# Regrouping the last stages of a fused attention and expert kernel: tiles 6, 7, 8 together, then 7, 8

## The chip, the cores and the metric

The kernel runs on 1 core of one Trainium2 chip. The metric is the device time of one execution in microseconds (us); lower is better. The engines are PE (matrix multiply, with its weight loads shown apart as PEld), DVE (vector), ACT (scalar), POOL (GpSimd) and SP, whose queue here only issues DMAs.

## What is computed

Three layers in float32, one after the other, on 1152 tokens (2 batches of 576) with 512 features:

```python
scores = scale * np.matmul(q, k.transpose(0, 1, 3, 2))          # 8 heads of 64
kth = np.partition(scores, -32, axis=-1)[..., -32:-31]           # the 32 largest of a row stay
attn = softmax(np.where(scores >= kth, scores, -1e9))
x = attn @ v
...
for e in range(4):                                               # all four experts, gated
    out += p[:, e:e + 1] * (np.maximum(x @ w1[e], 0.0) @ w2[e])
...
h = np.maximum(np.maximum(x @ w1, x @ w2), x @ w3)               # second network
return h @ w_out
```

The weights of the last network (m1, m2, m3, mo) arrive as float64 and are turned into float32 on the chip.

## The kernel before

The 1152 tokens are nine tiles of 128. Attention goes over 36 pairs (a tile and two heads), and a table of slots (`options`, constants FIRST, TIGHT and LOOSE at L35 to L37) says at which slot each step of a pair is issued: scores on PE, four rounds of MAX8 and MATCH_REPLACE8 on DVE, exp on ACT, masking on DVE or (pairs in ON_POOL) on POOL, transposes and the product with v on PE. Tiles 0 and 1 take whole float32 operands (`kfull`, `qfull`, and `first_alone` for the experts of tile 0); the later ones are split into a high and a low float32r part, and each product is three matmuls (`product`, L616 to L618).

Between these slots the generator `products` issues expert work. How much is issued after a slot is set by two counted clocks: the goal grows with the DVE time counted, times SHARE, and products are issued until PE's counted time has reached it. All engines take their instructions in the order in which they are written; nothing is reordered later.

Expert work goes by stages (`STAGES`). Stage c covers a short list of tiles and only half of the weights (`HALVES`: weight halves 0 to 3 in even stages, 4 to 7 in odd ones), so every tile stands in one even and one odd stage: stage 0 is tile 0 alone, stages 1 to 8 are [0, 1], [1, 2] to [7, 8], and stage 9 is tile 8 alone. One weight half of a stage is layer 1 (`half1`: 16 products, 48 matmuls, with as many columns as the stage has tokens), and one item later layer 2 (`half2`: 4 products, 12 matmuls of 512 columns for each tile). A stage thus needs 16 weight tiles of 512 KB. Each comes by a DMA on SP's queue into `raw` (3 buffers, L186), is rounded to `whi` by ACT (L235), and `wlo` is the difference, two POOL instructions, or from stage LATE = 8 on for every second tile one DVE instruction (L241). A stage can start when its newest tile has left attention.

From slot W_FROM = 306 on, when attention ends, the 48 pieces of the second network's weights are converted (`to_float32`: two ACT, three DVE and one POOL instruction, L206 to L218, then a DMA to DRAM, L223), one piece every two slots. The second network (`largest`) then takes three groups of three tiles; its weight tiles come from that DRAM copy (`raw<-narrow`), nine for its first layer (ps) and three for its second (pso).

The queue of SP also carries attention's loads: `qraw` (one buffer) and `kraw` (one buffer), each twice, L283.

The lines that set the stages:

```python
STAGES = [[0]] + [[t - 1, t] if t % RING else [t, t - 1] for t in range(1, NTILE)] + [[NTILE - 1]]
HALVES = [range(E) if not n % 2 else range(E, 2 * E) for n in range(len(STAGES))]
```

Of the kernel before, what the change touches and what calls it, by code (L numbers as in the profile page):

```python
# [22 lines left out]
RING = 4  # L23
# [7 lines left out]
ON_POOL = ((0, 1, 2, 3, 4, 5, 6, 7), (0, 1, 2, 3, 4, 5, 6))  # L31
W_FIRST, W_AHEAD = 60, 4
# [20 lines left out]
def kernel(  # L53
# [72 lines left out]
    def load_gates():  # L126
        nc.scalar.dma_start(out=gate, in_=gates)
# [178 lines left out]
    def load_q(c, hp):  # L306
        t = qraw[c, hp] = qp.tile([P, 2, WIDTH], F32, tag="qraw", bufs=1, name="qraw")
# [40 lines left out]
    class Pair:  # L348
# [136 lines left out]
        def split_x(self):  # L485
# [8 lines left out]
            at_ = self.t % RING * P  # L494
# [4 lines left out]
    def attention():  # L499
# [5 lines left out]
        def options(n):  # L505
            return FIRST if n < EARLY else TIGHT if n == EARLY else LOOSE
# [6 lines left out]
        for n, (c, hp, t) in enumerate(pairs):  # L513
# [8 lines left out]
            elif n:  # L522
                at_slot(8 * n + options(n)["scores"] - LOAD_FULL, load_full, n)
# [46 lines left out]
        for n in range(len(HALVES[0]) * 2 + 2):  # L570
# [114 lines left out]
    def first_alone():  # L685
# [3 lines left out]
        for e in range(len(HALVES[0]) // 2):  # L689
# [16 lines left out]
            load_alone(14 + 2 * e)  # L706
        flush()
        for e, h in hs.items():
            ps = po.tile([P, DM], F32, tag="o", name="ps2")
            for y in range(2):  # L710
                for u in range(2):
                    w = w_alone["b", 2 * e + y, u]
                    for f in range(2):
# [3 lines left out]
                        yield True  # L717
            later(gated(ps, 0, e, not e, False))
        flush()

    def experts():
# [29 lines left out]
        def half2(c, i, hs, ti):  # L751
            t = STAGES[c][ti]
            if not i % 2:
                outs[t] = po.tile([P, DM], F32, tag="o", name="ps2")
# [5 lines left out]
            new = c < NTILE and t == c  # L760
            if new and t not in accs:
                sums(t)
                first = True
            else:
                first = False
            later(*[lambda: None] * E_LAG, gated(ps, t, i // 2, first, not new and i == HALVES[c][-1]))

        before = None
        for c in range(1, len(STAGES)):
            phase[0] = c  # L770
            newest = min(c, NTILE - 1)
# [9 lines left out]
            for i in HALVES[c]:  # L781
# [6 lines left out]
                if i == HALVES[c][-1]:  # L788
                    x_free.update(t for t in STAGES[c] if t != c)
# [195 lines left out]
```

## Time and profile before

| what | us |
|---|---|
| median of 3 runs | 830.49 (830.01 to 836.0) |
| the profiled execution itself | 830.46 |
| its span, first to last instruction | 828.7 |
| PE busy | 766.3 (92%) |
| DVE busy | 664.5 (80%) |
| POOL busy | 580.5 (70%) |
| ACT busy | 492.8 (59%) |

The span is what the rows further down cut into stretches; the 1.8 us between it and the execution's time lie outside the instructions. Busy time of PE is that of overlapping matmuls, whose ends are modelled, so PE at 100% is not PE at its peak; for the pace of matmuls the starts are counted instead.

### The profile page before, as it was taken

To read this page: it belongs to the slowest core of one execution; us is meant where nothing else is said; L and a number is where in the kernel's file an instruction comes from. 1 tells how busy PE (TensorE), PEld (TensorE's weight loads), DVE (VectorE), ACT (ScalarE), POOL (GpSimd) and SP (SyncE) were. 2 spreads that over 40 slices of the span, in tenths; PEclk is the share of its full clock that TensorE was granted. 3 is DMA by queue.
4 is the path that set the end of the run, shared out by engine and by line. 5 is a ranking of instruction groups with operands and counts; after the bars stand their busy time and mean duration, and the time that the engine had idled before them with its cause. 6 is when DMAs were issued, how large, how long until landed. Compare 5 with 4: busy or idle time off the path is not lost. (4 is left out here: it accounts for less than half of the span.)

```text
span 828.7 us, 14306 instructions
## 1 busy us (share of the span) xinstructions
PE 766.3 (92%) x4950; PEld 675.6 (82%) x4950; DVE 664.5 (80%) x1226; ACT 492.8 (59%) x1046; POOL 580.5 (70%) x487
## 2 busy tenths in 40 slices
PE   5988899998999999999999999899999797899998
PEld 3667578887888999888998988688888696699996
DVE  6999698997789998988999987899986886144141
ACT  4566757784677676757777766556655643243341
POOL 2668858886898878869879868997876763163330
PEclk9889999999999999999999999999997899799999
DMA  7743525545546555445455436789878763452431
GB/s 212 217 135 124 151 75 160 170 131 163 151 129 185 151 156 163 118 128 163 141 161 149 147 120 203 230 255 286 279 242 277 249 212 105 165 193 87 153 114 39
DMA packets 58376, 138.58 MB, mean 167 GB/s; under 512 B 9984, under 2 KB 23296, under 8 KB 58304
## 3 DMA queue, kind: packets, MB, share of 16 engines
q1 hardware_dynamic: 49792, 128.93, 50.6%
q10 hardware_dynamic: 8512, 8.74, 3.0%
q8 instruction: 39, 0.64, 0.3%
q14 instruction: 33, 0.27, 0.1%
HBM read 128.99 MB, written 8.65 MB: 166 GB/s over the span
## 5 line engine op out<-in xcount | busy, mean ns | idle before, releaser
L241 POOL TENSOR_TENSOR wlo<-raw,whi 128x512 fp32r<-128x512 f32 x290 | 390.9, 1374 | 133.4 <-ACT whi L235 127.8
L235 ACT ACTIVATE whi<-raw 128x1024 fp32r<-128x1024 f32 x180 | 188.0, 1060 | 111.8 <-DMA raw<-in_w_dram 64.8
L616 PE MATMUL ps<-xl,whi 128*128 128x256 f32 (+2 forms) x648 | 190.5, 294 | 3.2 <-ACT r L461 3.2
L618 PE MATMUL ps<-xh,wlo 128*128 128x256 f32 (+2 forms) x648 | 188.1, 290 | 1.4 <-POOL wlo L241 1.4
L617 PE MATMUL ps<-xh,whi 128*128 128x256 f32 (+2 forms) x648 | 188.0, 290 | 0.0
L393 DVE MAX8 m<-work 128x8 f32<-128x576 f32 x216 | 154.7, 743 | 0.1
L616 PEld LDWEIGHTS ps<-xl,whi 128*128 128x128 f32 x648 | 123.7, 191 | 5.3 <-ACT r L461 3.9
L618 PEld LDWEIGHTS ps<-xh,wlo 128*128 128x128 f32 x648 | 124.1, 192 | 1.7 <-POOL wlo L241 1.7
L617 PEld LDWEIGHTS ps<-xh,whi 128*128 128x128 f32 x648 | 124.1, 191 | 1.0
L616 PE MATMUL ps<-wlo,h 128*128 128x512 f32 x272 | 111.9, 411 | 5.8 <-POOL wlo L241 4.0
L618 PE MATMUL ps<-whi,h 128*128 128x512 f32 x272 | 108.8, 400 | 2.8 <-POOL h L737 2.8
L241 DVE TENSOR_TENSOR wlo<-raw,whi 128x1024 fp32r<-128x1024 f32 x35 | 51.8, 1481 | 72.8 <-ACT whi L235 61.6
L617 PE MATMUL ps<-whi,h 128*128 128x512 f32 x272 | 108.1, 397 | 0.0
L395 DVE MATCH_REPLACE8 work<-m,work 128x576 f32<-128x576 f32 x144 | 106.5, 741 | 0.0
L616 PEld LDWEIGHTS ps<-wlo,h 128*128 128x128 f32 x272 | 52.4, 193 | 18.4 <-POOL wlo L241 6.4
L413 DVE SCALAR_TENSOR_TENSOR p<-s,m,p 128x576 f32<-128x576 f32 x57 | 66.9, 1174 | 0.0
L218 POOL TENSOR_TENSOR narrow<-narrow,raw 128x256 int32<-128x256 int32 x48 | 46.0, 961 | 29.2 <-issue 9.6
L618 PEld LDWEIGHTS ps<-whi,h 128*128 128x128 f32 x272 | 52.0, 191 | 16.3 <-POOL h L737 4.8
L380 ACT ACTIVATE s<-pss 128x288 f32<-128x288 f32 x144 | 51.6, 409 | 21.1 <-PE pss L373 11.1
L431 PE MATMUL psp<-ident,p 128*128 128x128 f32 x288 | 46.0, 284 | 15.4 <-DVE h L744 6.2
L617 PEld LDWEIGHTS ps<-whi,h 128*128 128x128 f32 x272 | 52.4, 192 | 8.8
L393 DVE MAX8 m<-s 128x8 f32<-128x576 f32 x72 | 54.1, 752 | 3.7 <-ACT rs L444 2.8
(97 smaller groups left out, 1515.8 us busy)
## 6 DMA issues: line engine op xcount, KB each, us to landing
raw<-in_w_dram SPq DMA_DIRECT2D x144, 512.0 KB, 4.0
raw<-narrow SPq DMA_DIRECT2D x36, 512.0 KB, 3.7
raw<-in_m_dram SPq DMA_DIRECT2D x36, 256.0 KB, 4.4
whole<-in_w_dram SPq DMA_DIRECT2D x16, 512.0 KB, 4.7
narrow<-narrow ACTq DMA_DIRECT2D x48, 128.0 KB, 3.7
kraw<-in_k_dram SPq DMA_DIRECT2D x16, 288.0 KB, 5.4
qraw<-in_q_dram SPq DMA_DIRECT2D x48, 64.0 KB, 2.5
raw<-in_mo_dram SPq DMA_DIRECT2D x12, 256.0 KB, 4.3
```

The source lines that it names most:

```text
L218: nc.gpsimd.tensor_tensor(out=out.bitcast(I32), in0=out.bitcast(I32), in1=last, op=ALU.add)
L235: nc.scalar.activation(out=hi, in_=raw, func=AF.Copy)
L241: on.tensor_tensor(out=lo[:, x], in0=raw[:, x], in1=hi[:, x].bitcast(F32), op=ALU.subtract)
L380: nc.scalar.activation(out=s[:, h, :], in_=halves[h][:, 0:SH], func=AF.Copy)
L393: nc.vector.max(m[:, 8 * r:8 * r + 8], src)
L395: nc.vector.match_replace(out=self.w[j], in_to_replace=m[:, 8 * r:8 * r + 8], in_values=src, imm_value=NEG)
L413: nc.vector.scalar_tensor_tensor(out=p, in0=s, scalar=kth, in1=p, op0=ALU.is_ge, op1=ALU.mult, accum_out=total)
L431: nc.tensor.transpose(ps[:, r * P:(r + 1) * P], self.p[:, part, part * TAIL + r * P:part * TAIL + (r + 1) * P], ident)
L616: nc.tensor.matmul(ps, lhsT=lh, rhs=rl, start=first, stop=False)
L617: nc.tensor.matmul(ps, lhsT=lh, rhs=rh, start=False, stop=False)
L618: nc.tensor.matmul(ps, lhsT=ll, rhs=rh, start=False, stop=last)
```

## The change

- Stages: 1 to 6 as before, then stage 7 is [6, 7, 8] and stage 8 is [7, 8]; stage 9 is gone. The slots of the ring that holds a tile's x move by one (`place`), so that the three tiles lie side by side. With three tiles a layer 1 pass is 384 columns wide and takes two PSUM banks, and the third output of layer 2 takes a bank of the same pool of six.
- The first stage's weights (`whole`): 13 instead of 10 are loaded ahead, three of them into the `raw` buffers; the rest, and the first loads and splits of stage 1, move from fixed slots into `first_alone`.
- `qraw` gets two buffers and shrinks from 384 to 256 columns a head.
- TIGHT is used for pairs 3 and 7 (before: 7 alone). The second head of pair 3 is masked on DVE, not POOL.
- SHARE is 1.0 throughout (before 1.03 from stage 2 on).
- Start: one DMA for q instead of two, the gates' DMA on SP, the ACT table load (`warm`) behind the first DMA issue.

```diff
-ON_POOL = ((0, 1, 2, 3, 4, 5, 6, 7), (0, 1, 2, 3, 4, 5, 6))
-W_FIRST, W_AHEAD = 60, 4
+ON_POOL = ((0, 1, 2, 3, 4, 5, 6, 7), (0, 1, 2, 4, 5, 6))
+W_AHEAD = 4
...
-SHARE, AHEAD = (1.0, 1.0, 1.03), 6
+SHARE, AHEAD = (1.0, 1.0, 1.0), 6
...
-PHASES = [(1, n) for n in range(10)] + [(2, 0), (2, 1), (2, 2)]
+PHASES = [(1, n) for n in range(9)] + [(2, 0), (2, 1), (2, 2)]
...
+    def place(t):
+        return (t - 1) % RING
+
-    STAGES = [[0]] + [[t - 1, t] if t % RING else [t, t - 1] for t in range(1, NTILE)] + [[NTILE - 1]]
+    STAGES = [[0]] + [[t - 1, t] for t in range(1, NTILE - 2)] + [[NTILE - 3, NTILE - 2, NTILE - 1], [NTILE - 2, NTILE - 1]]
+    STAGES = [sorted(x, key=place) for x in STAGES]
...
-            t = wp.tile([P, 1024], F32, tag=("hi", "lo")[len(w_alone) % 2], name="whole")
+            n_ = len(w_alone)
+            tag, bufs = ("raw", 3) if 10 <= n_ < 13 else (("hi", "lo")[n_ % 2 if n_ < 10 else (n_ - 13) % 2], 5)
+            t = wp.tile([P, 1024], F32, tag=tag, bufs=bufs, name="whole")
...
-        t = qraw[c, hp] = qp.tile([P, 2, WIDTH], F32, tag="qraw", bufs=1, name="qraw")
+        t = qraw[c, hp] = qp.tile([P, 2, 2 * P], F32, tag="qraw", name="qraw")
...
-            return FIRST if n < EARLY else TIGHT if n == EARLY else LOOSE
+            return TIGHT if n in (HP - 1, 2 * HP - 1) else FIRST if n < 2 * HP else LOOSE
...
-        for n in range(len(HALVES[0]) * 2 + 2):
+        for n in range(13):
             at_slot(ALONE_FROM + ALONE_STEP * n, load_alone, n + 1)
...
-            load_alone(14 + 2 * e)
+            load_alone(16)
...
+                    if not e:
+                        w_load_to(2 * y + u)
+                    else:
+                        w_split_to(2 * y + u + 1)
...
-                outs[t] = po.tile([P, DM], F32, tag="o", name="ps2")
+                outs[t] = po.tile([P, DM], F32, tag="o", name="ps2") if ti < 2 else bank("ps2")
...
-    load_full(0, slice(0, 1), nc.scalar)
-    load_full(0, slice(1, 2), nc.scalar)
-    load_gates()
+    load_full(0, nc.scalar, load_gates)
+    warm_up()
+    norm_gates()
     for s, done in attention():
-        if s == W_FIRST - 12:
-            w_load_to(3)
-        if W_FIRST <= s < W_FIRST + 16 and not (s - W_FIRST) % 4:
-            w_split_to((s - W_FIRST) // 4 + 1)
```

Three places in the order of instructions, each before and after.

SP's queue where the first split heads are loaded (whole: weights of stage 0; raw: weights of the later stages; kraw, qraw: attention's k and q for splitting). Before:

```order
L283 DMA kraw<-in_k_dram 64x1152 x2
L186 DMA raw<-in_w_dram 128x1024 x3
L283 DMA qraw<-in_q_dram 64x2x128 x2
L260 DMA whole<-in_w_dram 128x1024 x4
L283 DMA kraw<-in_k_dram 64x1152 x2
L283 DMA qraw<-in_q_dram 64x2x128 x2
L260 DMA whole<-in_w_dram 128x1024 x2
L283 DMA kraw<-in_k_dram 64x1152 x2
```

The second load of k stands behind a qraw with one buffer and four weight tiles. After:

```order
L299 DMA kraw<-in_k_dram 64x1152 x2
L274 DMA whole<-in_w_dram 128x1024 x3
L299 DMA qraw<-in_q_dram 64x2x128 x2
L299 DMA kraw<-in_k_dram 64x1152 x2
L299 DMA qraw<-in_q_dram 64x2x128 x2
L299 DMA kraw<-in_k_dram 64x1152 x2
L198 DMA raw<-in_w_dram 128x1024 x3
```

Three weight tiles now stand ahead of the qraw, none between it and the second k, and the three raw have moved behind two more loads of q and k.

PE at the end of attention. Before, from the last transpose of attention (psr) on (ps with 256 columns: layer 1 of stage 7):

```order
L476 MATMUL psv<-pt,vt 64x128 x8
L459 MATMUL psr<-ident,rb 128x128
L616 MATMUL ps_6485<-xl,whi 128x256
L617 MATMUL ps_6485<-xh,whi 128x256
L618 MATMUL ps_6485<-xh,wlo 128x256
```

By then 1176 layer 1 and 552 layer 2 matmuls of the split stages have been issued, 24 of them already in stage 7. After, 36 matmuls behind the last psr, the end of stage 6 (512 columns) and the start of stage 7 (384 columns):

```order
L634 MATMUL ps_6426<-wlo,h 128x512
L635 MATMUL ps_6426<-whi,h 128x512
L636 MATMUL ps_6426<-whi,h 128x512
L634 MATMUL ps_6460<-xl,whi 128x384
L635 MATMUL ps_6460<-xh,whi 128x384
L636 MATMUL ps_6460<-xh,wlo 128x384
```

At the last psr the counts are 1140 and 528: 36 layer 1 and 24 layer 2 matmuls fewer lie inside attention. All 36 that follow it are of stage 6, and then the wide passes begin.

ACT in the second network's first group, where the last conversions stand (narrow<-raw and raw<-raw: the two ACT steps of a piece; DMA narrow: its write; whi: rounding of a weight tile; tm, hh: layer 1 drained; xh<-pst: the next group's tiles). Before:

```order
L206 ACTIVATE narrow<-raw_8477 128x256
L207 ACTIVATE raw_8477<-raw_8477 128x256
L862 ACTIVATE hh<-tm 128x768
L818 ACTIVATE xh<-pst 128x4x128
L223 DMA narrow_109<-narrow 128x256
L818 ACTIVATE xh<-pst 128x4x128
L223 DMA narrow_109<-narrow 128x256 x3
L235 ACTIVATE whi<-raw 128x1024 x3
```

The last piece is converted when layer 1 of this group has ended, and the three weight tiles of its second layer come behind it. After:

```order
L218 ACTIVATE narrow<-raw_8038 128x256
L219 ACTIVATE raw_8038<-raw_8038 128x256
L247 ACTIVATE whi<-raw 128x1024
L235 DMA narrow_106<-narrow 128x256
L247 ACTIVATE whi<-raw 128x1024
L235 DMA narrow_106<-narrow 128x256 x2
L881 ACTIVATE hh<-tm 128x768
L247 ACTIVATE whi<-raw 128x1024
L876 ACTIVATE tm<-ps_8157 128x384
L876 ACTIVATE tm<-ps_8174 128x384
L235 DMA narrow_106<-narrow 128x256
L247 ACTIVATE whi<-raw 128x1024
```

The last piece now stands ahead of the last third of layer 1 (tm<-ps_8157 opens it), and the weight tiles of the second layer come between its passes. In all 8 pieces are left for this group after its tiles have been turned (x2h), where there were 12.

## Rows read from the trace of the kernel before

**Rows 1.** Stretches: from:to, length, busy us of PE, PEld, DVE, ACT, POOL (instructions), clock, DMA, GB/s

```profile
12.00:82.00 70.00, 58.62 (x332) 43.87 (x332) 69.97 (x154) 42.56 (x123) 48.13 (x36) 0.88 0.57 177
82.00:100.00 18.00, 14.40 (x78) 9.81 (x77) 10.97 (x25) 12.99 (x32) 14.68 (x13) 0.91 0.60 157
100.00:502.45 402.45, 387.45 (x2868) 345.52 (x2867) 369.98 (x773) 275.77 (x617) 326.43 (x274) 1.00 0.49 146
502.45:655.27 152.82, 137.66 (x830) 120.18 (x830) 133.10 (x158) 91.34 (x161) 123.39 (x101) 0.95 0.80 255
655.27:697.09 41.82, 41.82 (x228) 41.78 (x229) 35.12 (x52) 19.77 (x41) 26.02 (x22) 0.93 0.59 187
697.09:722.41 25.32, 16.99 (x57) 12.63 (x56) 5.31 (x9) 6.67 (x9) 6.46 (x6) 0.73 0.43 146
```

**Rows 2.** Timeline of DVE, ACT and SP's queue near 85 us: start, length, [idle before <-releaser]

```profile
87.49 0.29 DVE L483 TENSOR_TENSOR xt<-psv,r 128x128 f32<-128x128 f32 x1 [4.21 <-ACT r L461]
...
86.04 1.26 ACT L294 ACTIVATE kT<-kraw 128x576 fp32r<-128x576 f32 x2 [5.27 <-DMA kraw<-in_k_dram]
...
74.62 1.96 SPq L260 DMA_DIRECT2D whole<-in_w_dram  x4
76.68 1.16 SPq L283 DMA_DIRECT2D kraw<-in_k_dram  x2
```

**Rows 3.** Waits of SP's queue from 20 to 120 us: us in total, times, longest

```profile
SPq L283 <- POOL ql L321: 36.4, 3, 23.7
```

**Rows 4.** Timeline of DVE and ACT near 194 us

```profile
194.96 0.69 DVE L744 SCALAR_TENSOR_TENSOR h<-ps,h 128x512 fp32r<-128x512 f32 x1 [4.37 <-ACT h L742]
...
193.38 1.06 ACT L235 ACTIVATE whi<-raw 128x1024 fp32r<-128x1024 f32 x1 [7.79 <-DMA raw<-in_w_dram]
```

**Rows 5.** Waits of SP's queue from 100 to 505 us

```profile
SPq L283 <- POOL ql L321: 54.2, 20, 8.0
```

**Rows 6.** Waits from 502.45 to 655.27 us

```profile
ACT whi L235 <- DMA raw<-in_w_dram: 35.6, 30, 3.2
```

**Rows 7.** Timeline of PE where the second network's layers start

```profile
655.27 0.69 PE L616 MATMUL ps<-x2l,whi 128*128 128x384 f32 x1 [5.08 <-DVE x2l L819]
...
704.65 0.80 PE L616 MATMUL pso<-wlo,hh 128*128 128x512 f32 x1 [5.92 <-POOL wlo L241]
```

**Rows 8.** Stretches in which PE does one kind of matmul back to back, columns as in rows 1

```profile
505.40:510.87 5.47, 5.47 (x27) 4.50 (x26) 4.95 (x5) 4.09 (x8) 5.46 (x5) 1.00 0.37 134
550.89:556.65 5.76, 5.76 (x50) 5.76 (x48) 5.66 (x7) 3.15 (x5) 4.75 (x6) 1.00 0.81 247
601.29:606.72 5.43, 5.43 (x49) 5.32 (x47) 4.77 (x9) 3.46 (x6) 2.88 (x4) 1.00 0.86 228
722.41:760.60 38.19, 38.19 (x218) 38.15 (x217) 15.05 (x17) 15.77 (x20) 17.45 (x12) 1.00 0.47 158
```

**Rows 9.** Costliest groups of the whole run: count, busy us, mean ns of one, idle before

```profile
L241 POOL TENSOR_TENSOR wlo<-raw,whi 128x512 fp32r<-128x512 f32 x290 | 390.9, 1374 | 133.4 <-ACT whi L235 127.8
...
L209 DVE SCALAR_TENSOR_TENSOR raw<-narrow,raw 128x256 f32<-128x256 f32 x48 | 43.1, 898 | 1.7 <-ACT narrow L206 1.7
L215 DVE SCALAR_TENSOR_TENSOR narrow<-raw,narrow 128x256 uint32<-128x256 uint32 x48 | 42.0, 875 | 1.1
L212 DVE TENSOR_SCALAR narrow<-raw 128x256 uint32<-128x256 uint32 x48 | 34.3, 714 | 0.9
```

**Rows 10.** Timeline of the start: ACT, its queue, PE

```profile
0.73 1.28 ACT L109 ACT_TABLE_LOAD   x1 [0.73 <-PEq L964]
...
1.38 1.20 ACTq L273 DMA_DIRECT2D qfull<-in_q_dram  x2
```

**Rows 11.** Timeline of DVE and POOL near 555 us

```profile
553.62 0.41 DVE L209 SCALAR_TENSOR_TENSOR raw<-narrow,raw 128x256 f32<-128x256 f32 x1
555.20 1.55 DVE L209 SCALAR_TENSOR_TENSOR raw<-narrow,raw 128x256 f32<-128x256 f32 x1
...
555.18 2.73 POOL L241 TENSOR_TENSOR wlo<-raw,whi 128x512 fp32r<-128x512 f32 x2 [0.51 <-ACT whi L235]
```

More of the change, by code (lines that the diff above doesn't have):

```diff
@@ L89 @@
     WIDTH = P * MAXT
-    STAGES = [[0]] + [[t - 1, t] if t % RING else [t, t - 1] for t in range(1, NTILE)] + [[NTILE - 1]]
+    def place(t):
+        return (t - 1) % RING
+    STAGES = [[0]] + [[t - 1, t] for t in range(1, NTILE - 2)] + [[NTILE - 3, NTILE - 2, NTILE - 1], [NTILE - 2, NTILE - 1]]
+    STAGES = [sorted(x, key=place) for x in STAGES]
     HALVES = [range(E) if not n % 2 else range(E, 2 * E) for n in range(len(STAGES))]
+    FIRST_IN = {t: min(n for n, x in enumerate(STAGES) if t in x) for t in range(NTILE)}
+    LAST_IN = {t: max(n for n, x in enumerate(STAGES) if t in x) for t in range(NTILE)}
+    assert all(set(x for n in range(len(STAGES)) if t in STAGES[n] for x in HALVES[n]) == set(range(2 * E)) for t in range(NTILE))
     const = ctx.enter_context(tc.tile_pool(name="const", bufs=1))
@@ L105, with warm_up @@
     make_identity(nc, ident)
-    warm = const.tile([P, 1], F32, name="warm")
-    nc.gpsimd.memset(warm, 0.0)
-    nc.scalar.activation(out=warm, in_=warm, func=AF.Exp)
+    def warm_up():
+        warm = const.tile([P, 1], F32, name="warm")
+        nc.gpsimd.memset(warm, 0.0)
+        nc.scalar.activation(out=warm, in_=warm, func=AF.Exp)
     clock = {"dve": 0.0, "pe": 0.0, "goal": AHEAD}
@@ L124, with load_gates, norm_gates @@
     gate = const.tile([P, NTILE, E], F32, name="gate")
-    def load_gates():
-        nc.scalar.dma_start(out=gate, in_=gates)
+    def load_gates(loaded=[]):
+        if not loaded:
+            nc.sync.dma_start(out=gate, in_=gates)
+            loaded.append(True)
+    def norm_gates():
         gs = const.tile([P, NTILE], F32, name="gs")
@@ L269, in rows, with load_full @@
         return slice(n % 2 * D, (n % 2 + 1) * D)
-    def load_full(n, heads=slice(0, 2), queue=nc.sync):
+    def load_full(n, q_queue=nc.sync, between=lambda: None):
         c, hp, t = pairs[n]
-        queue.dma_start(out=qfull[rows(n), heads], in_=q[hp, :, heads, t * P:(t + 1) * P])
-        nc.sync.dma_start(out=kfull[rows(n), heads], in_=k[0, hp][:, heads])
+        q_queue.dma_start(out=qfull[rows(n)], in_=q[hp, :, :, t * P:(t + 1) * P])
+        for heads in (slice(0, 2),) if n else (slice(0, 1), slice(1, 2)):
+            nc.sync.dma_start(out=kfull[rows(n), heads], in_=k[0, hp][:, heads])
+            between()
     v_last = [const.tile([P, P], F32, name="v_last%d" % i) for i in range(6)]
@@ L329, in xs_of @@
     def xs_of(tiles):
-        at_ = sorted(t % RING for t in tiles)
-        step = at_[-1] - at_[0] or 1
+        at_ = [place(t) for t in tiles]
+        step = max(1, at_[-1] - at_[0]) // max(1, len(at_) - 1)
+        assert at_ == list(range(at_[0], at_[-1] + 1, step))
         return [[x[:, a].rearrange("p (s n) -> p s n", n=P)[:, at_[0]:at_[-1] + 1:step] for a in range(KT)] for x in xring]
@@ L759, in half2 @@
                 return
-            new = c < NTILE and t == c
-            if new and t not in accs:
+            first = t not in accs
+            if first:
                 sums(t)
[L763 to L766, printed above, removed]
+            later(*[lambda: None] * E_LAG, gated(ps, t, i // 2, first, c == LAST_IN[t] and i == HALVES[c][-1]))
         before = None
@@ L770, in experts @@
             phase[0] = c
-            newest = min(c, NTILE - 1)
+            newest = max(STAGES[c])
             if c == 1:
@@ L788, in experts @@
                 if i == HALVES[c][-1]:
-                    x_free.update(t for t in STAGES[c] if t != c)
+                    x_free.update(t for t in STAGES[c] if LAST_IN[t] == c)
                 if before is not None:
```

5 lines of the change are left out of this document (3 added, 2 removed).

## The prediction

> **What bounds the kernel now.** I read the stretches first, then what ends the idle time in each, then the pace of the matmuls. The stretches [rows 1] split the span in three. From 12 to 82 us DVE is busy 69.97 of 70.00 us: the top-k of the first pairs sets the time, and PE waits for it. From 100 to 502.45 us PE is busy 387.45 of 402.45 us and DVE 369.98: PE leads, but DVE is close behind. From 502.45 us, when attention has ended, to 722.41 us no engine is full all the time: PE has 137.66 of 152.82 us, then 41.82 of 41.82, then only 16.99 of 25.32 us, and the mean clock granted to it in that last stretch is 0.73, a mix of its two levels (1.2 and 2.4 GHz) after it had stood idle.
>
> Between these lie stalls that belong to no engine's own work. From 82 to 100 us DVE works 10.97 of 18.00 us, so 7.0 us are lost in a part that DVE sets. One of the waits is shown [rows 2]: DVE waits 4.21 us for ACT, which waited 5.27 us in order for the transfer of kraw; that transfer was issued at 76.68 us behind four weight tiles of 512 KB. All of them came late because SP's queue had stood for up to 23.7 us at a load of qraw, whose one buffer POOL had not yet freed [rows 3]. The same happens later on a smaller scale: at 194 us DVE waits 4.37 us for ACT, which stood 7.79 us at a weight tile [rows 4], and SP's queue waits 54.2 us in 20 places for qraw's buffer [rows 5].
>
> In the tail ACT waits 30 times, 35.6 us in all, for weight tiles from DRAM [rows 6]. The second network starts after a PE wait of 5.08 us, and its second layer after one of 5.92 us for a weight tile whose conversion was last [rows 7].
>
> **What each part costs.** Pace of the matmuls, from stretches of one kind, counted by their starts [rows 8]: 24 of 512 columns in 5.47 us, 228 ns each; 48 of 256 columns in 5.76 us, 120 ns; 48 of 128 columns in 5.43 us, 113 ns; 216 of 384 columns in 38.19 us, 177 ns. Half the columns cost nearly the whole price, and PEld is busy almost as long as PE in the three narrower kinds: the loads of weights set their pace.
>
> Stages on PE. Stage 9's layer 1 goes: 4 halves of 48 matmuls, 192 x 113 ns = 21.7 us. Stage 7's 192 grow from 256 to 384 columns: 192 x (177 - 120) ns = 10.9 us. Layer 2 has as many matmuls as before. PE saves 10.8 us.
> The Trainium skill (TensorE: Matmul & The Clock Gate, Back-to-back issue gap) gives an isolated matmul N/2.4 + 2.5 ns and says that it counts too little at small N, with 81 ns measured at N = 128. By the formula the step would be 192 x (162.5 - 109.2 - 55.8) ns, a gain of under 1 us, and the forecast would be some 10 us higher; the row has 113 ns, above both, and decides.
>
> Where the 10.8 us appear. At the last psr 36 layer 1 and 24 layer 2 matmuls fewer have been issued: 36 x 120 ns + 24 x 228 ns = 9.8 us of PE work leave the stretch 100 to 502 us. If PE alone set it, it would shrink by 9.8 us, if DVE did, by nothing. PE has 15.0 idle us there, DVE 32.5: I take half, 5 us. In the tail up to the second network PE has left before: 360 x 120 + 192 x 113 + 264 x 228 ns = 125.1 us; after: 204 x 120 + 192 x 177 + 288 x 228 ns = 124.1 us. So 1 us goes there.
>
> The tail's stalls. The 152.82 us of the stretch hold 125.1 us of matmuls at full pace, so 27.7 us are waits, slow clock and 12 transposes. Stage 9 asked for 16 weight tiles in 192 x 113 + 48 x 228 ns = 32.6 us of PE time, 2.0 us each, where POOL alone takes 2 x 1.374 = 2.75 us for one that it subtracts [rows 9]; stages 7 and 8 asked for 16 in 192 x 120 + 96 x 228 ns = 44.9 us. After, stage 7 needs 16 in 192 x 177 + 144 x 228 ns = 66.8 us, and stage 9's 16 are not loaded, rounded or subtracted at all. On POOL stage 7 holds 16 x 2.75 = 44 us of subtractions and some 20 conversion steps, so it fits in 66.8, where it did not in 44.9. I take 10 us off; the bounds are 20 us (about all but the wait for x2l) and a loss of 5 us (pieces come denser: 38 before the second network's first load in 124 us of PE work, where 36 had 125).
>
> The second network's second layer: its 54 matmuls take 12.3 us at full pace, the stretch is 25.32 us [rows 1]; the other 13.0 us are waits, slow clock and 12 transposes. The last piece now stands ahead of the last third of layer 1, 72 x 177 ns = 12.7 us of PE earlier, which is about what its write, reload, rounding and subtraction need. I take 9 us off; bounds 0 and 12.
>
> The front. With two buffers qraw no longer stops SP, and no weight tile stands between it and the second k. 7.0 us were lost; the mask of pair 3 moves to DVE and costs it one more instruction, and the first splits of stage 1 come one to two pairs later, when POOL is freer, but with less lead. I take 5 us; bounds 0 and 7. The weight that came late at 194 us: 4 us of 4.37; bounds 0 and 4.4.
> The start: the ACT table load, 1.28 us, stood ahead of the first DMA issue at 1.38 us, which can now begin at 0.73 us [rows 10]: 0.6 us. Where the table load then lies, ACT has nothing to do until the first scores.
>
> Edits at nothing: SHARE is already counted in the matmuls that left attention; the shift of ring slots and the third output in the other bank pool change no count, and cost only by a wait (second rival).
>
> Sum: 0.6 + 5 + 4 + 5 + 1 + 10 + 9 = 34.6 us off the profiled 830.46 us, which is the median of 830.49 within 0.1 us: **796 us**.
>
> **Rivals.** First: the tail is set by the conversions, not by weights. The second layer's first weight tile waits for the last piece, so the 48 pieces take about from 502.45 us to its start at 704.65 us [rows 7], 4.2 us each. Each costs DVE 898 + 875 + 714 ns = 2.49 us [rows 9], 119 us in all, beside its other work. If their pace stays, the second layer starts no earlier relative to attention's end, and only 0.6 + 5 + 4 + 5 us are won: 816 us. For it: a DVE step of 0.41 us takes 1.55 us when a POOL subtraction of 2.73 us began just before [rows 11], and pieces get denser. Against it: DVE is idle 19.7 us of 152.82 [rows 1], and ACT's waits for weights are the longer item [rows 6].
> The Trainium skill (SBUF — State Buffer, Who interferes with whom) says that a DVE instruction with two SBUF inputs is blocked for the whole of a POOL instruction that reads SBUF, and not just slowed. The trace agrees: 1.55 us against 0.41 us. By that rule each POOL subtraction saved also shortens DVE, which speaks for the forecast; and where POOL subtracts through all of stage 7, it holds DVE back, which speaks for this rival.
>
> Second, slower: the wide stage chokes on PSUM. Each of its 8 layer 1 passes takes two of six banks, and the third output one more for two halves; a bank comes free only when DVE, in order behind the conversions, has drained it. If each pass waits for two pieces, 8 x 2 x 2.49 = 40 us are added, and the gains of the tail's stalls, the second layer and the shorter attention fall away: 830.5 - 10.6 + 40 = 860 us. It turns the result slower by over 1% from 2.4 us a pass on, (8.3 + 10.6) / 8. Against it: the second network's first layer also takes two banks a pass beside conversions, and PE is busy 41.82 of 41.82 us there [rows 1].
>
> Third: the front edits do not do what they say, because SP is stopped by something else (the moved weight tiles now wait for PE, and the loads of q and k behind them). Without 5 + 4 us it is 805 us. With the first rival too, 825 us, within 1%.
>
> **How the numbers follow.** Forecast 0.70, first rival 0.12, third 0.08, first and third together 0.06, second 0.04. A difference under 1% (8.3 us) is about what a measurement can't tell from none. Faster by over 1% holds for the forecast, the first and the third: 0.90; within 1% 0.06; slower 0.04. Range: with 20 instead of 10 us of the tail's stalls, 12 for 9 and 7 for 5 the sum is 49.6 us, 781 us; I put the low end at 780. The high end takes in the first rival, 816 us. What lies outside is the pair of rivals, the slow case and some of the low side.
>
> **What would show it.** Right: the DVE wait near 85 us gone and attention ended near 488 us; 192 layer 1 matmuls fewer, and 192 of 384 columns at about 177 ns in stage 7; the second layer's first wait under 2 us; ACT's waits for weight tiles in the tail well under 35.6 us. First rival: the last conversion still some 200 us after attention, PE waiting for pso. Second: PE waits in stage 7 ended by DVE's h. Wrong altogether: attention's end later than 502 us, or more than 10 us of new PE waits in stage 7.

## The result, and the profile after

The kernel after takes 789.78 us (median of 4 runs, 788.74 to 791.34), the kernel before 831.57 us beside it (830.01 to 836.0): ratio 0.9491, 95% interval 0.9449 to 0.9533. The forecast was 796 us with a range of 780 to 816. The profiled execution took 789.28 us, its span is 787.5 us. The page of the kernel after, busy time, clock and two of its groups:

```profile
span 787.5 us, 13848 instructions
PE 737.6 (94%) x4758; PEld 652.8 (83%) x4758; DVE 657.1 (83%) x1220; ACT 474.5 (60%) x1026; POOL 555.3 (71%) x467
PEclk9978999998999999999999999999999999999999
L253 POOL TENSOR_TENSOR wlo<-raw,whi 128x512 fp32r<-128x512 f32 x274 | 371.6, 1384 | 117.0 <-ACT whi L247 111.3
L253 DVE TENSOR_TENSOR wlo<-raw,whi 128x1024 fp32r<-128x1024 f32 x27 | 41.6, 1542 | 61.2 <-ACT whi L247 49.9
```

PE lost 28.7 us of busy time. POOL does 274 halves of wlo where it did 290 [rows 9], and the granted clock stays at nine tenths or more in every slice behind the 10th.

The stretches of the kernel after, cut where those of [rows 1] are cut: the eighth psr, the last psr, the first matmul on x2l, the first of pso, the next group. The last line is one wide layer 1 pass of stage 7:

```profile
12.00:82.00 70.00, 57.64 (x346) 44.19 (x347) 69.85 (x155) 42.87 (x124) 45.25 (x34) 0.90 0.58 177
82.00:98.10 16.10, 16.10 (x90) 9.77 (x90) 15.49 (x34) 13.31 (x37) 13.55 (x12) 1.00 0.51 149
98.10:487.50 389.40, 372.15 (x2779) 334.72 (x2778) 361.46 (x764) 269.61 (x605) 319.35 (x268) 0.98 0.50 149
487.50:628.37 140.87, 128.90 (x700) 111.74 (x698) 135.19 (x163) 82.40 (x158) 115.51 (x97) 1.00 0.75 237
628.37:669.16 40.79, 40.79 (x228) 40.75 (x229) 30.18 (x45) 18.14 (x31) 23.31 (x20) 0.96 0.59 204
669.16:681.84 12.68, 12.68 (x58) 10.22 (x56) 3.37 (x6) 4.45 (x7) 2.55 (x2) 1.00 0.33 120
508.28:516.61 8.33, 8.33 (x50) 8.32 (x49) 8.23 (x11) 3.85 (x7) 8.33 (x8) 1.00 0.78 250
```

What stood between 82 and 100 us is gone: DVE works 15.49 of 16.10 us, where it worked 10.97 of 18.00. The tail is 140.87 us for 152.82, and its clock 1.00 for 0.95. The last stretch but one took 25.32 us at a clock of 0.73 and takes 12.68 us at 1.00: PE is never idle in it. The wide pass has 48 matmuls in 8.33 us, 174 ns each.

The waits of the kernel after between 487.5 and 628.37 us, in total, times, longest:

```profile
ACT whi L247 <- DMA raw<-in_w_dram: 23.5, 17, 3.7
...
PE ps L634 <- DVE x2l L838: 3.9, 1, 3.9
PE ps L634 <- POOL wlo L253: 2.8, 3, 1.2
PE ps L636 <- POOL hl L759: 1.9, 2, 1.3
```

ACT's waits for weight tiles fell from 35.6 us in 30 places [rows 6] to 23.5 us in 17. The wide stage brought no long PE wait. Where the second network's two layers start (timeline of PE):

```profile
628.37 0.44 PE L634 MATMUL ps<-x2l,whi 128*128 128x384 f32 x1 [3.87 <-DVE x2l L838]
...
669.16 0.48 PE L634 MATMUL pso<-wlo,hh 128*128 128x512 f32 x1
```

The first wait is 3.87 us for 5.08, the second, 5.92 us before [rows 7], does not exist. One place that answers to [rows 4], ACT and DVE near 190 us, has not changed:

```profile
189.88 0.69 DVE L766 SCALAR_TENSOR_TENSOR h<-ps,h 128x512 fp32r<-128x512 f32 x1 [4.45 <-ACT h L764]
188.31 1.06 ACT L247 ACTIVATE whi<-raw 128x1024 fp32r<-128x1024 f32 x1 [6.99 <-DMA raw<-in_w_dram]
```

DVE waits 4.45 us there, as it waited 4.37 us before.

### The profile page after: what moved, and what is told of

Read it like the earlier page. It is cut to its first block, busy times and chain, and to the rows that moved or that the text cites. A ratio compares the mean times of both kernels' runs of the same rounds, so it can differ in the third digit from the quotient of the medians.

```text
span 787.5 us, 13848 instructions
## 1 busy us (share of the span) xinstructions
PE 737.6 (94%) x4758; PEld 652.8 (83%) x4758; DVE 657.1 (83%) x1220; ACT 474.5 (60%) x1026; POOL 555.3 (71%) x467
## 4 chain that ended last, share of the span: by engine, by line
PE 47%; DVE 15%; DMA 8%; ACT 6%; issue 3%; POOL 3%; SPq 0%; ACTq 0%; DVEq 0%; POOLq 0%
PE ps L634 11%; PE ps L636 11%; PE ps L635 11%; DMA raw<-in_w_dram 5%; DVE m L410 4%; DVE work L412 3%; PE pss L390 3%; ACT whi L247 2%; PE psv L493 2%; POOL wlo L253 2%; PE psp L448 2%; DMA narrow<-narrow 2%; PE pso L635 2%; PE pso L636 2%; PE pso L634 2%
## 5 line engine op out<-in xcount | busy, mean ns | idle before, releaser
L253 POOL TENSOR_TENSOR wlo<-raw,whi 128x512 fp32r<-128x512 f32 x274 | 371.6, 1384 | 117.0 <-ACT whi L247 111.3
L247 ACT ACTIVATE whi<-raw 128x1024 fp32r<-128x1024 f32 x164 | 171.1, 1061 | 75.2 <-DMA raw<-in_w_dram 43.9
L634 PE MATMUL ps<-xl,whi 128*128 128x256 f32 (+1 forms) x584 | 174.8, 299 | 3.6 <-ACT acc L698 2.0
L635 PE MATMUL ps<-xh,whi 128*128 128x256 f32 (+1 forms) x584 | 171.6, 294 | 0.0
L636 PE MATMUL ps<-xh,wlo 128*128 128x256 f32 (+1 forms) x584 | 171.6, 294 | 0.0
L634 PE MATMUL ps<-wlo,h 128*128 128x512 f32 x224 | 90.9, 406 | 3.1 <-POOL wlo L253 1.2
L636 PE MATMUL ps<-whi,h 128*128 128x512 f32 x224 | 88.4, 395 | 1.5 <-POOL h L759 1.5
L635 PE MATMUL ps<-whi,h 128*128 128x512 f32 x224 | 88.2, 394 | 0.0
L448 PEld LDWEIGHTS psp<-ident,p 128*128 128x128 f32 x288 | 35.7, 147 | 25.9 <-POOL p L434 8.9
L423 ACT ACTIVATE p<-s,nb 128x576 f32<-128x576 f32 x72 | 55.7, 774 | 0.0
L412 DVE MATCH_REPLACE8 work<-m,s 128x576 f32<-128x576 f32 x72 | 53.2, 739 | 0.0
```

Of the source, the lines that this page charges most:

```text
L247: nc.scalar.activation(out=hi, in_=raw, func=AF.Copy)
L253: on.tensor_tensor(out=lo[:, x], in0=raw[:, x], in1=hi[:, x].bitcast(F32), op=ALU.subtract)
L412: nc.vector.match_replace(out=self.w[j], in_to_replace=m[:, 8 * r:8 * r + 8], in_values=src, imm_value=NEG)
L423: nc.scalar.activation(out=self.p[:, j].rearrange("p (a n) -> p a n", a=2), in_=self.s[j], func=AF.Exp, bias=self.nb[j], scale=SCALE)
L448: nc.tensor.transpose(ps[:, r * P:(r + 1) * P], self.p[:, part, part * TAIL + r * P:part * TAIL + (r + 1) * P], ident)
L634: nc.tensor.matmul(ps, lhsT=lh, rhs=rl, start=first, stop=False)
```

## The experiments

Each kernel's trace gives the same marks by its timeline of PE. In us: the eighth psr; the length from there to the last psr (attention); from there to the first matmul on x2l (tail); from there to the end of the first group's second layer (two layers); and how far the last conversion step on POOL ends ahead of the first pso (a minus: behind it).

| kernel | median | eighth psr | attention | tail | two layers | lead |
|---|---|---|---|---|---|---|
| before | 831.57 | 103.4 | 399.0 | 152.9 | 67.1 | -4.7 |
| before_share | 824.93 | 104.3 | 389.0 | 168.0 | 54.4 | 11.7 |
| stages_alone | 809.21 | 103.6 | 396.4 | 135.8 | 66.2 | -4.3 |
| old_stages | 817.26 | 98.2 | 390.1 | 168.5 | 53.6 | 9.4 |
| share_103 | 799.15 | 99.7 | 392.2 | 132.8 | 65.6 | -4.3 |
| one_qraw | 793.72 | 99.4 | 394.5 | 141.9 | 52.0 | 9.5 |
| old_loads | 790.89 | 100.0 | 387.4 | 141.3 | 53.8 | 11.3 |
| both_undone | 791.58 | 100.8 | 388.5 | 141.3 | 53.8 | 10.9 |
| front_undone | 798.33 | 103.5 | 391.9 | 141.7 | 53.6 | 11.0 |
| after | 789.78 | 98.1 | 389.4 | 140.9 | 53.5 | 10.6 |
| share_split | 790.17 | 98.4 | 391.9 | 138.4 | 56.6 | 11.1 |
| late_7 | 784.45 | 99.3 | 390.0 | 137.2 | 52.1 | 9.2 |
| half_columns | 831.35 | 104.0 | 399.0 | 153.9 | 66.4 | -4.6 |
| no_dve_conv | 819.69 | 103.3 | 399.2 | 146.2 | 62.8 | 2.6 |

### The regrouping, undone and alone

old_stages is the kernel after with the old stages:

```diff
-    STAGES = [[0]] + [[t - 1, t] for t in range(1, NTILE - 2)] + [[NTILE - 3, NTILE - 2, NTILE - 1], [NTILE - 2, NTILE - 1]]
+    STAGES = [[0]] + [[t - 1, t] for t in range(1, NTILE)] + [[NTILE - 1]]
-PHASES = [(1, n) for n in range(9)] + [(2, 0), (2, 1), (2, 2)]
+PHASES = [(1, n) for n in range(10)] + [(2, 0), (2, 1), (2, 2)]
```

> The changed kernel with the stages of before (stage 7 is [6, 7], 8 is [7, 8], 9 is tile 8 alone); all else as changed. If regrouping is worth what the two traces say (10.8 us of PE work, some 10 us of the tail's stalls, some 9 us before the second network's second layer, less what overlaps), this takes 812 to 820 us, and only attention's end, near 488 us, is as in the changed kernel. Rival: regrouping is worth its PE work alone and the rest came from the front, the queue and SHARE: 799 to 803 us.

Measured: 817.26 us, ratio to the kernel before 0.9835 (0.9814 to 0.9856). The regrouping is worth 27.5 us beside the other edits, all of it in the tail (168.5 to 140.9 us). stages_alone is the kernel before with the new stages and what they need (`place`, the last stage of a tile, the bank for the third output), and SHARE still 1.03:

```diff
-    STAGES = [[0]] + [[t - 1, t] if t % RING else [t, t - 1] for t in range(1, NTILE)] + [[NTILE - 1]]
+    STAGES = [[0]] + [[t - 1, t] for t in range(1, NTILE - 2)] + [[NTILE - 3, NTILE - 2, NTILE - 1], [NTILE - 2, NTILE - 1]]
...
```

> The kernel before with the new stages and nothing else of the change (SHARE 1.03, one qraw buffer, old loads). If the parts add up, this takes 803 to 810 us: the tail's gain in full, attention's end within 3 us of that of before (about 500 us). If the tail's gain needs the earlier end of attention or the calmer queue, 815 us or more.

Measured: 809.21 us, ratio 0.9735 (0.97 to 0.9769): 21 us without the other edits. Of these the tail has 17.1. The long PE wait in the second layer is still there (two layers 66.2 us), though the stages are the new ones. The two parts do not add up: the new stages alone gain 21 us and the other edits alone 13 us (old_stages against the kernel before beside it, 830.21 us), 34 together, where all edits at once gain 41.8.

### SHARE, in both directions

share_103 is the kernel after with the old third value of SHARE:

```diff
-SHARE, AHEAD = (1.0, 1.0, 1.0), 6
+SHARE, AHEAD = (1.0, 1.0, 1.03), 6
```

> The changed kernel with SHARE 1.03 from stage 2 on, so 12 layer 1 and 24 layer 2 matmuls (7 us) more lie ahead of attention's last psr. If PE sets the stretch from 100 us to attention's end, that end moves from 487.8 to 491 to 495 us and PE then has to wait for tile 8: 790 to 794 us in all. Rival, DVE sets that stretch: the end stays within 1 us of 487.8, and the time falls by up to 5 us, as 7 us of work were hidden.

Measured: 799.15 us, ratio 0.9617 (0.9588 to 0.9646), a miss: 9.4 us slower than after, not 0 to 4. The trace of share_103 at the end of the first layer (timeline of POOL and PE), its wait there, and the stretch from pso to the next group:

```profile
669.46 0.73 POOL L230 TENSOR_TENSOR narrow<-narrow,raw 128x256 int32<-128x256 int32 x1 [2.17 <-issue]
...
677.84 0.80 PE L634 MATMUL pso<-wlo,hh 128*128 128x512 f32 x1 [8.87 <-DVE wlo L253]
```

```profile
665.90:690.30 24.40, 15.53 (x57) 12.10 (x56) 5.11 (x7) 5.42 (x8) 4.63 (x5) 0.79 0.41 145
```

The last piece is converted at 670.19 us, 4.3 us after the first pso matmul; PE waits 8.87 us for a later weight tile of that layer and then runs at a low clock, 24.40 us in all. In the kernel after, the step that answers to it on POOL:

```profile
657.78 0.75 POOL L230 TENSOR_TENSOR narrow<-narrow,raw 128x256 int32<-128x256 int32 x1 [2.69 <-PE ps L636]
```

ends at 658.53 us, 10.6 us before pso starts. So the 12 us of the second layer hang on SHARE and not on the stages: the column of leads has the same split in every kernel with all steps of the conversion, 4 us behind with 1.03 and 9 us or more ahead with 1.0, whatever the stages are. The pieces stand at fixed slots; with a lower SHARE more products are left for those slots, and the last piece comes ahead of more of them.

before_share is the kernel before with the new value:

```diff
-SHARE, AHEAD = (1.0, 1.0, 1.03), 6
+SHARE, AHEAD = (1.0, 1.0, 1.0), 6
```

> The kernel before with SHARE 1.0 alone. The earlier runs suggest that SHARE, not the regrouping, ends the wait before the second network's second layer: that stretch (second network's start to the next group's) falls from 67 to 54 us, while 9.8 us of work move from attention into the tail, whose stages then take about 166 to 168 us instead of 153; attention ends 2 to 3 us earlier. In all 826 to 832 us, no gain without the regrouping. Rival, the wait goes and little else changes: 815 to 820 us.

Measured: 824.93 us, ratio 0.9899 (0.986 to 0.9939), 1 us under what was expected, and with a gain where none was expected: the kernel before had 832.71 us beside it, and the interval lies below 1. Attention ends 9.1 us earlier, not 2 to 3. Attention and the tail of before_share, in columns as above:

```profile
104.30:493.30 389.00, 373.78 (x2785) 335.34 (x2784) 360.91 (x764) 267.93 (x603) 314.07 (x264) 1.00 0.49 146
493.30:661.30 168.00, 150.57 (x892) 130.53 (x890) 147.32 (x172) 99.01 (x176) 135.26 (x114) 0.93 0.78 250
```

Attention is 10.0 us shorter, which is all of the 9.8 us of matmuls that left it (892 instead of 830 of them now stand in the tail, 62 more). PE's work set that stretch of the kernel before. In the tail the moved matmuls cost 15.1 us, and the two layers give 12.7 us back. The other way round it is less plain. share_103 puts 12 layer 1 and 24 layer 2 matmuls, 6.9 us at the pace of [rows 8], back ahead of attention's last psr, and attention grows by 2.8 us only:

```profile
99.74:491.99 392.25, 375.19 (x2814) 336.95 (x2812) 363.68 (x765) 271.81 (x606) 321.77 (x270) 1.00 0.51 151
```

Its clock there is 1.00, that of the kernel after 0.98. So PE's work does not set the length of attention one for one in the kernel after; how much of the difference is the clock's was not tried apart.

share_split tried to have both, 1.03 while attention runs and 0.95 in stage 7 and later:

```diff
-SHARE, AHEAD = (1.0, 1.0, 1.0), 6
+SHARE, AHEAD = (1.0, 1.0, 1.03, 1.03, 1.03, 1.03, 1.03, 0.95), 6
```

> The changed kernel with SHARE 1.03 for stages 2 to 6 and 0.95 from stage 7 on. The last piece then stands as early among the weight tiles as in the changed kernel (8 tiles into the second network), with 7 us more work ahead of attention's end. If the wait before the second layer hangs on the place of that piece, it stays away (second network's start to the next group's 54 us), attention ends 3 to 5 us later, the tail's stages take 7 to 8 us less: 784 to 788 us. Rival, SHARE in attention itself costs what share_103 lost: 795 us or more.

Measured: 790.17 us, ratio 0.9467 (0.9433 to 0.9501). This lies between the two answers expected, with no gain over the kernel after: the last piece does stay ahead (lead 11.1 us), but the tail is only 2.5 us shorter, where 7 to 8 were expected, attention is 2.5 us longer, and the two layers are 3.1 us longer, 2.9 of them in one PE wait for DVE's tm.

### What sets the tail

half_columns is the kernel before with 64 columns instead of 128 in 144 of stage 9's 192 layer 1 matmuls:

```diff
+                if N == P and a:
+                    (lh, ll), (rh, rl) = [w[:, a, f * P:(f + 1) * P] for w in wt], [x[a][:, :, 0:P // 2] for x in xs]
...
```

> The kernel before with 64 instead of 128 columns in three of four products of stage 9's layer 1, 144 of its 192 matmuls (half of the tokens' partial sums are left out there). If the loads of weights set the pace of 128 columns, the matmuls of 64 columns still start about 113 ns apart and a half without stall takes 5.4 us. Rival, the columns count: 27 ns less each, 4.5 us for a half and 1 us less in each of the four.

Measured: one run, 831.35 us; the kernel before had 832.71 beside it. Consecutive starts in its timeline of PE:

```profile
628.49 0.28 PE L652 MATMUL ps<-xh,whi 128*128 128x64 f32 x1
628.61 0.28 PE L653 MATMUL ps<-xh,wlo 128*128 128x64 f32 x1
...
629.27 0.28 PE L653 MATMUL ps<-xh,wlo 128*128 128x64 f32 x1
```

Seven steps from start to start in 0.78 us are 111 ns each, with half the columns of [rows 8] at 113 ns. So the columns do not set the pace of a narrow matmul, and the regrouping saves whole matmuls at nearly full price, as the forecast had it. That the load of its weights is what a narrow matmul pays for is likely, but not shown: PEld is as busy at 384 columns (38.15 of 38.19 us, [rows 8]), where the pace is 177 ns, and no run changed the loads. The formula of the Trainium skill (TensorE: Matmul & The Clock Gate, Back-to-back issue gap) would give 64/2.4 + 2.5, an estimate of 29 ns. The section says itself that the formula counts too little at small N; the trace, at 111 ns, agrees with that and lies above the section's 81 ns for 128 columns too.

no_dve_conv is the kernel before without the three DVE instructions of each converted piece (L209, L212, L215), their count in the clock kept:

```diff
-        nc.vector.scalar_tensor_tensor(out=hf, in0=out, scalar=LEAST, in1=hf, op0=ALU.is_ge, op1=ALU.mult)
...
-        nc.vector.tensor_scalar(out=t, in0=high, scalar1=3, scalar2=0x3FFFFFF8, op0=ALU.logical_shift_left, op1=ALU.bitwise_and)
...
-        nc.vector.scalar_tensor_tensor(out=t, in0=high, scalar=0xC0000000, in1=t, op0=ALU.bitwise_and, op1=ALU.bitwise_or)
```

> The kernel before without the three DVE instructions of each converted piece (the bits of the second network's weights are not put together); ACT, POOL and all DMAs stay, and the order of the rest too. If weights set the tail's stages, the stretch from attention's end to the second network, 152.9 us, falls by under 5 us. If the conversions on DVE do (my first rival), by 15 us or more, to 138 us or less, near the 126 us of matmuls and transposes.

Measured: one run, 819.69 us. Its tail:

```profile
502.60:648.80 146.20, 132.24 (x832) 114.97 (x830) 46.74 (x52) 91.51 (x161) 116.67 (x102) 0.99 0.83 263
```

DVE falls from 133.10 to 46.74 us of the stretch and the stretch by 6.7 us only. This lies between the two answers expected: DVE's conversions are a part of the tail's cost and do not set it alone. The whole run is 13.0 us shorter than the kernel before beside it, as the two layers lose 4.3 us as well. What else there is can be read in the kernel before, PE alone, where stage 9 runs:

```profile
624.20 0.33 PE L618 MATMUL ps<-xh,wlo 128*128 128x128 f32 x1 [0.91 <-POOL wlo L241]
625.62 0.33 PE L618 MATMUL ps<-xh,wlo 128*128 128x128 f32 x1 [0.54 <-POOL wlo L241]
...
634.51 0.63 PE L616 MATMUL ps<-wlo,h 128*128 128x512 f32 x1
634.94 0.63 PE L617 MATMUL ps<-whi,h 128*128 128x512 f32 x1
```

```profile
624.00:626.00 2.00, 1.27 (x9) 1.00 0.98 366
626.00:628.00 2.00, 2.00 (x15) 0.71 0.74 175
628.00:630.00 2.00, 2.00 (x11) 0.50 0.98 332
...
636.00:638.00 2.00, 2.00 (x9) 0.73 0.55 185
638.00:640.00 2.00, 2.00 (x21) 1.00 1.01 309
```

(columns: length, PE busy and matmuls, granted clock, DMA share, GB/s.) PE waits twice for POOL's wlo between 623 and 626 us, 1.45 us together, and for 0.49 us at 620 us. Then the clock stands at 0.50, the lower of its two levels (1.2 GHz of 1.2 and 2.4), from about 627 to 637 us, in which PE is never idle, and a matmul of 512 columns starts every 0.43 us instead of 0.228. About 5 us are lost in these 10, more than in the waits ahead of them.

late_7 is the kernel after with every second wlo on DVE from stage 7 on:

```diff
-LATE = 8
+LATE = 7
```

> The changed kernel with LATE = 7: every second weight tile of stage 7 is subtracted by DVE (one instruction) instead of POOL (two). If POOL sets what is left of stage 7's waits, the stretch from attention's end to the second network falls from 140.9 us by 2 to 5 us: 785 to 788 us. Rival, DVE with its conversions is as full as POOL there: no change within 2 us, or up to 5 us slower.

Measured: 784.45 us (782.26 to 786.1), ratio 0.9406 (0.9373 to 0.9439), an interval below that of the kernel after: the fastest kernel here. Its tail and the wait of PE for POOL in it:

```profile
489.30:626.50 137.20, 130.73 (x699) 114.10 (x697) 129.48 (x171) 81.77 (x158) 94.64 (x81) 0.98 0.77 244
```

```profile
PE ps L634 <- POOL wlo L253: 0.7, 1, 0.7
```

POOL has 94.64 us of work in place of 115.51, PE waits 0.7 us for it in place of 2.8, and the tail is 3.7 us shorter. In the wide pass of the kernel after that is shown above, POOL was full (8.33 of 8.33 us) and DVE nearly so (8.23). Yet DVE, which took on 8 more subtractions (18 wlo in the tail, where it had 10), is busy 5.7 us less, 129.48 for 135.19 us. The same 40 conversion steps became shorter, here the first of the three, in the tail of the kernel after and of late_7 (count, busy us, mean ns):

```profile
L221 DVE SCALAR_TENSOR_TENSOR raw<-narrow,raw 128x256 f32<-128x256 f32 x40 | 38.5, 962 | 0.5 <-ACT narrow L218 0.3
...
L221 DVE SCALAR_TENSOR_TENSOR raw<-narrow,raw 128x256 f32<-128x256 f32 x40 | 29.4, 734 | 0.1
```

This fits [rows 11], where such a step takes 1.55 us for 0.41 beside a POOL subtraction: with fewer of those, DVE's own steps take less time. The two were not tried apart, as late_7 changes the work of both engines.

### What shortened the front

one_qraw is the kernel after with one buffer for qraw:

```diff
-        t = qraw[c, hp] = qp.tile([P, 2, 2 * P], F32, tag="qraw", name="qraw")
+        t = qraw[c, hp] = qp.tile([P, 2, 2 * P], F32, tag="qraw", bufs=1, name="qraw")
```

> The changed kernel with one qraw buffer. If the waits of SP's queue for that buffer cost what I took (most of 5 us at the front, 4 us later), this takes 794 to 800 us, and DVE's waits near 85 us and near 194 us come back, with ACT waiting for kraw and weight tiles. Rival, the order of the loads alone cured the front, as no weight tile stands ahead of the second k any more: within 2 us of the changed kernel.

old_loads has the weights of the first stage, and the first loads and splits of stage 1, in their old places:

```diff
-            tag, bufs = ("raw", 3) if 10 <= n_ < 13 else (("hi", "lo")[n_ % 2 if n_ < 10 else (n_ - 13) % 2], 5)
-            t = wp.tile([P, 1024], F32, tag=tag, bufs=bufs, name="whole")
+            t = wp.tile([P, 1024], F32, tag=("hi", "lo")[len(w_alone) % 2], name="whole")
...
+        if s == 60 - 12:
+            w_load_to(3)
+        if 60 <= s < 60 + 16 and not (s - 60) % 4:
+            w_split_to((s - 60) // 4 + 1)
```

> The changed kernel with the old schedule of the first stage's weights (10 buffers, stage 1's loads and splits at fixed slots); two qraw buffers, TIGHT for pair 3 and the new start stay. If the order of these loads on SP's queue cured the front, the eighth psr moves back from 98.1 us to 102 or 103 us and the whole takes 793 to 796 us. Rival, the two qraw buffers or the tighter chain of pair 3 did: within 2 us of the changed kernel, the eighth psr before 100 us.

Measured: 793.72 us, ratio 0.9554 (0.9527 to 0.9581), and 790.89 us, ratio 0.9485 (0.9453 to 0.9518). The first lies between the answers expected, the second fits its rival. The eighth psr comes 1.3 and 1.9 us later, not 4 or more, and old_loads regains it by the end of attention. Either could cover for the other, so both_undone takes both edits back:

> The changed kernel with one qraw buffer and the old schedule of the first stage's weights together. One alone moved the eighth psr from 98.1 us by only 1.3 and 1.9 us. If either of the two cures the front, undoing both brings the stall near 85 us back: the eighth psr at 102 to 104 us, DVE waiting 4 us or more there, and with the 5 us that one buffer costs later 797 to 802 us in all. Rival, the tighter chain of pair 3 or the new start cured the front: the eighth psr stays under 101 us and the time near that of one buffer alone, 793 to 796 us.

Measured: 791.58 us, ratio 0.9491 (0.9465 to 0.9518): 2.7 us at the eighth psr and 1.8 us in the time, which the ratios, 0.9491 for both kernels, do not resolve. The time is under both answers expected; the eighth psr fits the rival. The reading that these two cure the front fell here. front_undone takes back, beside these two, TIGHT for pair 3 and its mask on DVE:

```diff
-            return TIGHT if n in (HP - 1, 2 * HP - 1) else FIRST if n < 2 * HP else LOOSE
+            return FIRST if n < EARLY else TIGHT if n == EARLY else LOOSE
-ON_POOL = ((0, 1, 2, 3, 4, 5, 6, 7), (0, 1, 2, 4, 5, 6))
+ON_POOL = ((0, 1, 2, 3, 4, 5, 6, 7), (0, 1, 2, 3, 4, 5, 6))
```

> The kernel after with one buffer for qraw, the first weights in their old order, and also pair 3 back in FIRST with its second head masked on POOL; only the new start (one DMA for q, gates on SP, table load behind the first issue) stays of the edits to the front. With only the first two undone the eighth transpose of attention came at 100.8 us (after 98.1, before 103.4). If TIGHT for pair 3 is what else shortens the front, the eighth transpose comes at 102 to 104 us, DVE has waits of 4 us or more near 85 us again, and the run takes about 2 us more than with the two edits undone, 792 to 796 us. If the gain that is left is the new start's alone, the eighth transpose stays at 101 us or earlier and the time at 790 to 792 us.

Measured: 798.33 us (797.75 to 798.91), ratio 0.9595 (0.9553 to 0.9638), over what was expected of it and 6.7 us over both_undone; the eighth psr is at 103.5 us, where the kernel before has 103.4, so the new start that is left brings nothing at this mark. The timeline of front_undone shows the wait of [rows 2] again, DVE, ACT and SP's queue:

```profile
87.60 0.29 DVE L498 TENSOR_TENSOR xt<-psv,r 128x128 f32<-128x128 f32 x1 [5.04 <-ACT r L476]
...
86.14 1.25 ACT L308 ACTIVATE kT<-kraw 128x576 fp32r<-128x576 f32 x2 [6.12 <-DMA kraw<-in_k_dram]
...
72.59 1.21 SPq L297 DMA_DIRECT2D qraw<-in_q_dram  x2
73.89 1.96 SPq L272 DMA_DIRECT2D whole<-in_w_dram  x4
75.94 1.19 SPq L297 DMA_DIRECT2D kraw<-in_k_dram  x2
```

and that of both_undone, where it is absent:

```profile
82.77 1.25 ACT L308 ACTIVATE kT<-kraw 128x576 fp32r<-128x576 f32 x2
...
65.80 1.77 SPq L272 DMA_DIRECT2D whole<-in_w_dram  x4
67.62 1.52 SPq L198 DMA_DIRECT2D raw<-in_w_dram  x3
73.62 1.21 SPq L297 DMA_DIRECT2D qraw<-in_q_dram  x2
76.82 1.12 SPq L297 DMA_DIRECT2D kraw<-in_k_dram  x2
```

In both, qraw has one buffer, SP stops at it and goes on near 73 us, and kraw is issued near 76 us. The difference is where the four weight tiles stand: between qraw and kraw, or in front of the stop, issued 8 us earlier. TIGHT has other slots for pair 3, and its loads of q and k stand elsewhere between the weights'. With the 2 MB out of its way kraw is there before ACT asks for it: it lands 9.3 us after its issue in front_undone and 4.1 us in both_undone (issues near 76 us: size, median us to landing):

```profile
kraw<-in_k_dram SPq DMA_DIRECT2D x2, 288.0 KB, 9.3
...
kraw<-in_k_dram SPq DMA_DIRECT2D x2, 288.0 KB, 4.1
```

That TIGHT does this and not the mask on DVE was not tried apart.

## Why the prediction was right, step by step

The time is 6.2 us under the forecast and within its range; the sum of the profiled executions is 41.2 us where 34.6 were forecast.

| term | forecast | measured by the marks |
|---|---|---|
| start | 0.6 | 0.8 (first matmul at 3.85 us for 4.62) |
| front, to the eighth psr | 5 | 4.5 (5.3 without the start's 0.8) |
| attention: late weight 4, moved work 5 | 9 | 9.6 |
| tail: PE work 1, stalls 10 | 11 | 12.0 |
| second network's first layer | 0 | 1.0 |
| its second layer | 9 | 12.6 |
| the rest | 0 | 0.6 |

**The front.** The row was read rightly: DVE waits for ACT, ACT in order for kraw, kraw behind four weight tiles. The step that failed is "with two buffers qraw no longer stops SP" as the reason: a single buffer left the gain nearly whole (both_undone). The other half of that sentence, no weight tile between qraw and the second k, carries it, and TIGHT for pair 3, with its mask on DVE, brings that when the two other edits are undone. The 0.8 us of the start are not shown to be the edit's: stages_alone, with the old start, has its first matmul at 3.99 us. Taken together the edits to the front that front_undone takes back are worth 8.5 us of the time (front_undone against after), close to the 9 that the third rival took away.

**Attention.** Two steps failed and cancel. "The weight that came late at 194 us: 4 us": it is still late, DVE still waits 4.45 us. "I take half, 5 us" of the moved work: before_share shows the whole, 10.0 of 9.8 us. PE, with 15.0 idle us of 402, was the bound; DVE, idle for 32.5 us, was not a second one, and its being close behind was no argument for half. That 4 and 5 add up to nearly the 9.6 measured is luck.

**The tail.** The matmuls' part was right: 174 ns for 177 forecast, and narrow ones that cost nearly the whole price. The reason given for it, PEld almost as busy as PE, was no evidence: it holds at 384 columns too, where the columns do set the pace. The stalls were sized well, 12.0 for 11 us, though by a sum of larger items: SHARE moved 9.8 us into the tail, and against that tail (old_stages) the regrouping takes 27.6 us off. Of these 10.8 are matmuls. PE's idle time falls from 19.2 us (168.50 less 149.26, the tail of old_stages) to 12.0 (140.87 less 128.90), 7.3 us. The other 9.6 us are busy time over the full pace, 149.26 less 134.9 (125.1 and 9.8) against 128.90 less 124.1. The clock accounts for most of it: 0.95 over 168.50 us is 8.4 us short of full, where the tail of the kernel after has 1.00. The forecast put "waits, slow clock" into one term and argued by POOL's waits alone; the clock is the larger item. Tail of old_stages, columns as above:

```profile
488.30:656.80 168.50, 149.26 (x892) 128.93 (x890) 145.22 (x172) 98.94 (x176) 135.22 (x114) 0.95 0.78 246
```

**The second layer.** 12.6 for 9 us, the upper bound 12 just passed. The mechanism (the last piece ahead of the last third of layer 1) is what the traces show; the step that failed is "Edits at nothing: SHARE". It was read as work moved out of attention, and it also sets how many products stand behind the last conversion. The 12 us are its doing, by share_103 and before_share, with the old stages as with the new. This is the term that the forecast missed most in its cause. The 1.0 us of the first layer, forecast at nothing, goes with its clock, 0.93 before and 0.96 after.

**The rivals.** The first, conversions that set the tail, does not hold: with a whole DVE load taken away the tail of the kernel before lost 6.7 us, where its test asked for 15 or more. Nor does the second layer keep its distance from attention's end: its first matmul comes 181.7 us behind it (669.16 less 487.50), where it came 194.6 us behind (697.09 less 502.45). Part of it was true, as 6.7 us is not nothing, and the wait in the second layer did hang on the last piece. The second did not come: the largest of such waits, for tiles made from a drained bank, is POOL hl with 1.9 us in two places, where it needed 40. The third is refuted by front_undone: the front edits bring their 8.5 us, if not by the edit that was named. Its premise did come true, as SP's queue in the kernel after stands up to 15.9 us at a weight tile that waits for PE, but DVE works 15.49 of 16.10 us up to the eighth psr all the same.

Still open: why one_qraw alone has 5 us more in attention, where both_undone has none (388.5 us); and TIGHT without any other edit to the front, which wasn't tried.

## What to carry to other kernels

A constant that paces one engine's work against another's also sets which instruction of a side job stands ahead of which product; count the order at the end of the program, not only the work that moved. When a wait for a DMA is found, look at what is issued just before that DMA on its queue, and test each edit that moves it, as one edit in a list can do the work of another. Count a short stall with what PE's clock does after it: waits of 0.91 and 0.54 us were followed by 10 us at half speed.

## What the runs showed of the hardware that was not expected

A float32r matmul of 64 columns starts no sooner after the one before than one of 128 columns (111 and 113 ns). And short waits of PE did not always lower its clock. In the kernel before it fell to 0.50 at about 627 us, behind waits of 0.49, 0.91 and 0.54 us between 619 and 626 us. In the kernel after, two longer waits near the end of the tail were not followed by a fall, as its clock is 1.00 over the whole tail; it fell only behind the third wait, of 3.87 us, when the second network had begun (timeline of PE, then a stretch of PE alone):

```profile
618.68 0.50 PE L634 MATMUL ps<-wlo,h 128*128 128x512 f32 x1 [0.99 <-ACT h L758]
620.56 0.50 PE L636 MATMUL ps<-whi,h 128*128 128x512 f32 x1 [1.15 <-POOL h L759]
...
630.00:632.00 2.00, 2.00 (x8) 0.50 0.97 287
```

The runs here don't settle what makes the difference.
